# Expert 1's tokens in the later experts' order of d: quarter gathers and VectorE transposes for its second lot

## The chip, the cores and the metric

The kernel runs on one core of a Trainium2 chip. The metric is device time in microseconds (us), the median of several executions. One further execution was taken with the hardware profiler. Its trace is what "the profile" and "the trace" mean below, and its times count from the first instruction of the span.

Engines: TensorE (PE; its weight loads are PEld), VectorE (DVE), ScalarE (ACT), GpSimd (POOL) and SyncE (SP). SP issues the plain DMAs on a hardware queue. POOL issues the indirect DMAs (gathers and scatters by a list of indices) on a software queue.

## The reference

Two stages. Linear attention: for each of 8 batches and 8 heads, kv = kᵀv, out = q·kv, then a root-mean-square norm over the 64 channels of the head, times g_norm. The heads side by side are x, 8 x 576 tokens of 512 channels. Then a mixture of 8 experts in which each token goes to one expert:

```python
for b in range(B):
    prev_e = -1
    for s in range(S):
        fresh_e = int(np.argmax(logits[b, s]))
        if s == 0 or local_gate[b, s] < 0.5:
            e = fresh_e
        else:
            e = prev_e if prev_e >= 0 else fresh_e
        prev_e = e
        ...                      # p = softmax(logits[b, s])
        h = np.maximum(x[b, s] @ w1[e], 0.0)
        out[b, s] = p[e] * (h @ w2[e])
```

w1 is 8 x 512 x 1024 and w2 is 8 x 1024 x 512, all float32.

## The kernel before, in words

**Attention.** 16 steps of four batches' head pairs write unnormalised rows of x, with their norm factors and gates beside them, to a scratch tensor xs in DRAM: 4608 rows of 584 numbers, which are four pieces of 146, one for each pair of heads. The routing of each token is worked out beside it, and the tokens of each expert are listed (indices gidr for reading, sidr for writing).

**Experts.** The eight experts run one after another; "expert r" is the r-th in the order of work. Expert 0 has four blocks of 128 tokens, the last two each run by `block`. Experts 1 to 7 are sorted by their number of tokens on the chip, with fixed capacities WIDTHS (768, 704, 640, ...), so which weights expert r has is known only when `ranks` has run; SP then reads the numbers into registers (`read_ranks`, L1122) and issues the loads.

**Precision.** Each float32 product is three TensorE products: the operands are split into a high part (written by ScalarE) and a low part (by VectorE): high x high, high x low, low x high (`split_mm`, L961, L966, L967).

**Weights.** Each expert has four pieces of w1 and four of w2, of 512 KB. `wload` fetches a piece into one of four staging buffers `wst` (`wfetch`, L186 in the profile); `wsplit` has ScalarE write the high part (L233 for w1 with its scale g_norm, L230 for w2) and VectorE the low part (L234, L231), and then asks for the next load, which waits for a free staging buffer. The w1 pieces of expert 1 are called w_4 to w_7 in the profile.

**Tokens.** A block's 128 rows are gathered by POOL into a tile `xr` (six of them, XB, in turn), scaled by the norm factors (`scale`, L808), turned so that d lies on the partitions, and split into xh and xl. There are two ways to do this. A *whole* block is gathered by one DMA of whole rows (`gather`, L770), turned by four TensorE transposes into PSUM and split from there (`turn`, L820, L824, L825). The other way gathers a quarter of the row at a time (`gather4`, L780, four DMAs): quarter n of the partitions gets, in the u-th DMA, the u-th group of 32 tokens, piece by piece; VectorE then transposes 32 x 32 squares (`turn4`, L797) and the d index comes out in another order. The weights w1 must then lie in that order too (`quarters`), so their piece is read as four runs of 32 rows. Before the change, expert 1's blocks are whole and those of experts 2 to 7 are not.

**The order of work around the change.** Each of experts 1 to 7 has two lots of blocks, la and lb. Expert 1 has three blocks in each. For a lot, `first_wide` makes the first layer of all its blocks at once, in eight chunks of twelve products, with three PSUM buffers `ph`; ScalarE (L1031, hh) and VectorE (L1032, hl) take each chunk out. Then `second` makes the second layer block by block, ScalarE scales the result into one of two buffers `ot` (L996), and POOL scatters it to the output (L997). Lists of small jobs (`then`, `hooks`, `todo`) are written between the chunks: weight splits, scalings, turns of the next lot, and gathers of the lot after that, one per tick. For all engines but SP the program keeps the order in which it is written.

Expert 1's la is gathered, scaled and turned during `block` of expert 0's fourth block, and its w1 pieces are split there, at points given by its hooks. lb is gathered behind that, its blocks are scaled in the last three chunks of la's `first_wide`, and turned in la's second layer.

Of the kernel before, what the change touches and what calls it, by code (L numbers as in the profile page):

```python
# [11 lines left out]
I32 = mybir.dt.int32  # L12
# [10 lines left out]
def kernel(  # L23
# [12 lines left out]
    nc = tc.nc  # L36
    P = 128
# [69 lines left out]
    sidx = const.tile([P, KBM], I32, name="sidx")  # L107
    gidr = const.tile([P, NR * KBM], I32, name="gidr")

    gid4 = const.tile([P, NP, NR * KBM - KBM], I32, name="gid4")  # L110
    quart = const.tile([P, 2], F32, name="quart")
    own4 = const.tile([P, NP], F32, name="own4")
    nc.gpsimd.memset(own4, 0.0)
# [85 lines left out]

    def wload(e, i):  # L200
        t = wpools["w"].tile([P, 2 * DM], F32, name="wst", bufs=4)
        wfetch(t, by[e], i, e > 1)
        staged[e, i] = t

    by = {0: 0}
# [34 lines left out]
    def wsplit(e, i, two=False):  # L240
        t = staged.pop((e, i))

        if i < NW1:
            slot = (e * NW1 + i) % (2 * NW1)
            nm, pool = f"w1_{slot}", "s" if slot < NW1 else "b"
        else:
            slot = (e * NW2 + i - NW1) % (NW2 + 2)
            nm, pool = f"w2_{slot}", "scc"[slot] if slot < 3 else "d" if slot < NW2 else "b"
        hi, lo = (wtile(pool, nm + x) for x in "hl")
        low_ = split_w(hi, lo, t, i, e > 1)  # L250
        wt[e, i] = (hi, lo)

        def low(engine=nc.vector):
            low_(engine)
            if to_load:
                wload(*to_load.pop(0))

        if two:
            return low
        low()  # L260
# [388 lines left out]

    def by_quarter():  # L650

        n = NR * KBM - KBM
        pq4 = rbank[:, 128:128 + NP * n].rearrange("p (u n) -> p u n", n=n)
        for u in range(NP):
            nc.tensor.matmul(pq4[:, u], sel[0][:, u], trs[0][:, KBM:], start=True, stop=True)
        t = sm.tile([P, NP, n], F32, name="q4", tag="co")
        nc.vector.tensor_scalar(t, pq4, float(NP), quart[:, 1:2], op0=ALU.mult, op1=ALU.add)
        nc.vector.tensor_scalar(gid4, t, quart[:, 0:1], None, op0=ALU.max)
# [119 lines left out]
    def gather4(xr, c, u):  # L778

        i = nc.gpsimd.indirect_dma_start(  # L780
            out=xr[:, u * PW:(u + 1) * PW], out_offset=None,
            in_=xs.rearrange("t (q w) -> (t q) w", w=PW),
            in_offset=bass.IndirectOffsetOnAxis(ap=gid4[:, u, c - KBM:c - KBM + 1], axis=0),
            bounds_check=NT * NP - 1, oob_is_err=False)
        if behind:
            tc.add_manual_dep(i.ins, behind.pop().ins.name, mybir.DependencyInfo(
                mybir.DependencyClass.NoSync, mybir.DependencyReason.DATA))
# [3 lines left out]
    def pieces(xr, o=XO, n=P):  # L791
        return xr[:, 0:NP * PW].rearrange("p (a w) -> p a w", w=PW)[:, :, o:o + n]
# [22 lines left out]
    def turn(xr, xh, xl, t0, psum, tag="pt", pin=False, late=False):  # L815

        pt = psum.tile([P, ND, P], F32, name="pt", tag=tag)
        xv = pieces(xr)
        for d in range(ND):
            i = nc.tensor.transpose(pt[:, d], xv[:, d], ident)  # L820
            if late and not d:
# [463 lines left out]
    def remaining(some):  # L1285

        with tc.If(some > 0, preferred_fallthrough_block=True):  # L1287
            with ExitStack() as ov:
# [2 lines left out]
                tails(op, n0, KST)  # L1291
                others(op)

    class Block:


# [13 lines left out]
            return [lambda u=u: one(u) for u in range(NP)]  # L1310

        def scale(self):
            scale(self.xr)
            n = 1 if self.whole else NP
            t = xp.tile([P, NP, NR], F32, name="gs", bufs=2)[:, 0:n]
            nc.vector.tensor_mul(t, pieces(self.xr, XG, NR)[:, 0:n],
# [6 lines left out]

        def turn(self, xh, xl, t0):
            if self.whole:
                turn(self.xr, xh, xl, t0, ps_t)
            else:
                turn4(xp, self.xr, xh, xl, t0)

# [3 lines left out]
    def parts(r):  # L1333

        n = WIDTHS[r - 1]
        na = HM if n > 2 * HM - P else 2 * P
        bl = [Block(r, k, min(P, n - k * P), r == 1) for k in range(-(-n // P))]
        return bl[:na // P], bl[na // P:], na, n - na

    assert "F" in done  # L1340
# [26 lines left out]

    with tc.manual_schedule(engines=order):
        for bl in lb:
            bl.gather()  # L1370
        for r in range(1, E):
            la, lb, na, nb = lots[r]
            ma, mb_ = lots[r + 1][:2] if r + 1 < E else ([], [])
# [89 lines left out]
```

## Time and profile before

| | |
|---|---|
| median of three runs | 580.54 us (579.57 to 580.59) |
| the profiled execution | 575.91 us, of which the span is 574.1 us |
| busy share of the span | PE 94%, PEld 84%, DVE 53%, ACT 41%, POOL 40% |
| granted TensorE clock | 0.98 in the mean |
| DMA | 94.96 MB, 165 GB/s in the mean |
| instructions | 12792 |

A row of the timeline has its start and its duration in us, engine, line, operation, out<-in by the program's names, shapes, and in brackets how long the engine idled before it and what released it. A group's row has the count, and the least, median and greatest duration in ns. In a row of windows the busy times of PE, PEld, DVE, ACT and POOL follow the window's length, each with a count of instructions, and then come the granted TensorE clock, the share of the 16 DMA engines that was busy, and GB/s. A DMA queue's row has packets, MB, and its packets' time as a share of 16 engines. "issue" as a releaser means that the profile shows nothing that the engine waited for.

The attention part takes about the first 124 us, expert 0 the stretch to about 178 us, and experts 1 to 7 the rest.

### The profile page before, as it was taken

To read this page: it belongs to the slowest core of one execution; us is meant where nothing else is said; L and a number is where in the kernel's file an instruction comes from. 1 tells how busy PE (TensorE), PEld (TensorE's weight loads), DVE (VectorE), ACT (ScalarE), POOL (GpSimd) and SP (SyncE) were. 2 spreads that over 40 slices of the span, in tenths; PEclk is the share of its full clock that TensorE was granted. 3 is DMA by queue.
4 is the path that set the end of the run, shared out by engine and by line. 5 is a ranking of instruction groups with operands and counts; after the bars stand their busy time and mean duration, and the time that the engine had idled before them with its cause. 6 is when DMAs were issued, how large, how long until landed. Compare 5 with 4: busy or idle time off the path is not lost. (4 is left out here: it accounts for less than half of the span.)

```text
span 574.1 us, 12792 instructions
## 1 busy us (share of the span) xinstructions
PE 538.0 (94%) x5157; PEld 481.0 (84%) x5157; DVE 303.2 (53%) x627; ACT 237.6 (41%) x435; POOL 232.1 (40%) x303
## 2 busy tenths in 40 slices
PE   2977987789999999999999999999999999999996
PEld 2866876679878989898898898989798979999894
DVE  1126676699686525635463746374536545564510
ACT  1667766572254233332434343433433333435220
POOL 4224333161245527334353673447344634532001
PEclk9989889799999999999999999999999999999998
DMA  7999899980676354233343453336234533432000
GB/s 222 342 372 341 306 324 348 346 293 25 239 254 219 122 180 134 71 103 103 120 117 120 128 139 109 126 123 176 80 135 134 142 104 132 135 105 78 18 20 30
DMA packets 41379, 94.96 MB, mean 165 GB/s; under 512 B 7263, under 2 KB 7263, under 8 KB 41312
## 3 DMA queue, kind: packets, MB, share of 16 engines
q1 hardware_dynamic: 32032, 72.64, 37.1%
q0 software_dynamic: 7744, 21.41, 12.5%
q8 instruction: 42, 0.69, 0.5%
q10 hardware_dynamic: 1536, 0.02, 0.1%
q14 instruction: 25, 0.20, 0.1%
HBM read 73.85 MB, written 20.86 MB: 165 GB/s over the span
## 5 line engine op out<-in xcount | busy, mean ns | idle before, releaser
L780 POOL DMA_INDIRECT xr<-xs,gid x120 | 133.5, 1112 | 36.6 <-issue 33.2
L1032 DVE SCALAR_TENSOR_TENSOR hl<-ph,hh 128x384 fp32r<-128x384 f32 (+3 forms) x92 | 52.3, 569 | 113.6 <-ACT hh L1031 110.2
L997 POOL DMA_INDIRECT out_dram<-ot,sidr x34 | 33.8, 994 | 176.1 <-ACT ot L996 134.1
L1031 ACT ACTIVATE hh<-ph 128x384 fp32r<-128x384 f32 (+3 forms) x92 | 46.9, 510 | 121.7 <-PE ph L967 121.7
L996 ACT ACTIVATE ot<-py,pe 128x512 f32<-128x512 f32 (+1 forms) x37 | 25.4, 687 | 70.1 <-PE py L967 31.6
L495 POOL TENSOR_TENSOR sq<-raw 128x576 f32<-128x576 f32 x16 | 18.5, 1159 | 58.4 <-ACT raw L465 51.5
L375 PE MATMUL po<-vt,kt 64*64 64x64 f32 x1152 | 26.1, 243 | 15.7 <-DMA vt<-in_v_dram 11.5
L375 PEld LDWEIGHTS po<-vt,kt 64*64 64x64 f32 x1152 | 23.8, 156 | 14.3 <-issue 9.7
L500 DVE TENSOR_REDUCE ms<-sq 128x9 f32<-128x576 f32 x32 | 22.8, 747 | 21.5 <-POOL sq L495 19.5
L456 PEld LDWEIGHTS po<-kvb,qT 64*64 64x64 f32 x1024 | 22.2, 144 | 11.6 <-issue 9.3
L456 PE MATMUL po<-kvb,qT 64*64 64x73 f32 x1024 | 27.3, 242 | 4.7 <-issue 4.6
L462 ACT COPY raw<-po 128x876 f32<-128x876 f32 (+1 forms) x32 | 20.7, 651 | 15.3 <-PE po L456 15.1
L396 POOL COPY kvb<-kvp 64x128 f32<-64x128 f32 x64 | 20.5, 321 | 12.4 <-ACT kvp L379 10.0
L808 DVE TENSOR_TENSOR xr<-xr 128x512 f32<-128x512 f32 x37 | 25.4, 686 | 0.0
L801 ACT CAST yh<-xT 128x512 fp32r<-128x512 f32 x17 | 10.5, 620 | 29.5 <-DVE xT L797 29.4
L961 PE MATMUL py<-w_1h,hh 128*128 128x512 f32 (+1 forms) x56 | 22.2, 397 | 0.0
L435 PE MATMUL pq<-ident,qt 128*128 128x128 f32 x128 | 20.4, 307 | 1.8 <-issue 1.7
L966 PE MATMUL py<-w_0l,hh 128*128 128x512 f32 (+1 forms) x56 | 22.1, 395 | 0.0
L967 PE MATMUL py<-w_0h,hl 128*128 128x512 f32 (+1 forms) x56 | 22.0, 393 | 0.1
L961 PE MATMUL py<-w_0h,hh 128*128 128x512 f32 (+1 forms) x56 | 22.0, 393 | 0.0
L966 PE MATMUL py<-w_1l,hh 128*128 128x512 f32 (+1 forms) x56 | 21.9, 391 | 0.0
L967 PE MATMUL py<-w_1h,hl 128*128 128x512 f32 (+1 forms) x56 | 21.9, 391 | 0.0
(433 smaller groups left out, 1660.2 us busy)
## 6 DMA issues: line engine op xcount, KB each, us to landing
wst<-in_moe_w_dram SPq DMA_DIRECT2D x64, 512.0 KB, 3.7
xs<-raw SPq DMA_DIRECT2D x36, 292.0 KB, 4.4
kt<-in_k_dram SPq DMA_DIRECT2D x32, 288.0 KB, 4.6
vt<-in_v_dram SPq DMA_DIRECT2D x32, 288.0 KB, 4.9
qt<-in_q_dram SPq DMA_DIRECT2D x32, 288.0 KB, 5.5
xr<-xs,gid POOLq DMA_INDIRECT x120, 4.3
out_dram<-ot,sidr POOLq DMA_INDIRECT x36, 4.4
xr<-xs,gidr POOLq DMA_INDIRECT x6, 6.6
```

The costliest lines, as they stand in the source:

```text
L375: nc.tensor.matmul(pk[half(x ^ b), x, 0:D], ks[b][half(x), cd], vs[b][half(x), cd], start=(c == 0), stop=(c == C - 1))
L456: nc.tensor.matmul(po[half(b), r, o:o + HW], lhsT[half(r), half(x)], kvb[half(r), slot(x, b):slot(x, b) + HW], start=True, stop=True)
L500: nc.vector.tensor_reduce(mss[g][:, :, 2 * n + x], sqs.pop((s, x)), axis=AX.X, op=ALU.add)
L780: i = nc.gpsimd.indirect_dma_start(out=xr[:, u * PW:(u + 1) * PW], out_offset=None, in_=xs.rearrange("t (q w) -> (t q) w", w=PW), in_offse ...
L808: (engine or nc.vector).tensor_mul(xv, xv, r.unsqueeze(3).to_broadcast([P, NP, 2, D]))
L961: mm = nc.tensor.matmul(ps, ah, bh, start=(first and i == 0), stop=False)
L966: nc.tensor.matmul(ps, ah, bl, start=False, stop=False)
L967: nc.tensor.matmul(ps, al, bh, start=False, stop=(last and i == n - 1))
L996: nc.scalar.activation(ot[0:m], po[0:m], AF.Copy, scale=pe[0:m])
L997: return nc.gpsimd.indirect_dma_start(out=outf, out_offset=bass.IndirectOffsetOnAxis(ap=idx[0:m], axis=0), in_=ot[0:m], in_offset=None, bo ...
L1031: nc.scalar.activation(hh, ps, AF.Relu)
L1032: nc.vector.scalar_tensor_tensor(hl, ps[:, :, 0:nl], 0.0, hh[:, :, 0:nl].bitcast(F32), op0=ALU.max, op1=ALU.subtract)
```

## The change

Expert 1's first lot stays whole: gathered by whole rows and turned on TensorE. Its scaling now writes a second tile, with d put into the later experts' order on the way (`scale_turned`, two products of 256 elements for each block in place of one of 512). Its second lot is now gathered in quarters and turned on VectorE, as all later lots are. The w1 loads of expert 1 therefore come in four runs of 32 rows, and its split takes the scale vector in that order (gq for gcol). The table of quarter indices grows by the three blocks of lb (39 columns for 36).

```diff
-    gid4 = const.tile([P, NP, NR * KBM - KBM], I32, name="gid4")
+    gid4 = const.tile([P, NP, NR * KBM - HM // P], I32, name="gid4")
...
-        wfetch(t, by[e], i, e > 1)
+        wfetch(t, by[e], i, e > 0)
...
-        low_ = split_w(hi, lo, t, i, e > 1)
+        low_ = split_w(hi, lo, t, i, e > 0)
...
-        n = NR * KBM - KBM
+        n = NR * KBM - HM // P
...
-            nc.tensor.matmul(pq4[:, u], sel[0][:, u], trs[0][:, KBM:], start=True, stop=True)
+            nc.tensor.matmul(pq4[:, u], sel[0][:, u], trs[0][:, HM // P:], start=True, stop=True)
...
-            in_offset=bass.IndirectOffsetOnAxis(ap=gid4[:, u, c - KBM:c - KBM + 1], axis=0),
+            in_offset=bass.IndirectOffsetOnAxis(ap=gid4[:, u, c - HM // P:c - HM // P + 1], axis=0),
...
-        xv = pieces(xr)
+        xv = xr if len(xr.shape) == 3 else pieces(xr)
...
+    def scale_turned(xr):
+
+        t = xtile(xp, XB)
+        tv = t[:, 0:DM].rearrange("p (x y a i) -> p x a y i", x=2, a=NP, i=QD)
+        xv = pieces(xr).rearrange("p a (x y i) -> p x a y i", x=2, i=QD)
+        r = pieces(xr, XR, 2)
+        for x in range(2):
+            nc.vector.tensor_mul(tv[:, x], xv[:, x], r[:, :, x:x + 1].unsqueeze(3).to_broadcast(
+                [P, NP, DM // P // 2, QD]))
+        return t[:, 0:DM].rearrange("p (d k) -> p d k", k=P)
...
         def scale(self):
-            scale(self.xr)
+            if self.whole:
+                self.xs = scale_turned(self.xr)
+            else:
+                scale(self.xr)
...
-                turn(self.xr, xh, xl, t0, ps_t)
+                turn(self.xs, xh, xl, t0, ps_t)
...
-        bl = [Block(r, k, min(P, n - k * P), r == 1) for k in range(-(-n // P))]
+        bl = [Block(r, k, min(P, n - k * P),
+                    r == 1 and k < na // P) for k in range(-(-n // P))]
...
         for bl in lb:
-            bl.gather()
+            for what in bl.gathers():
+                what()
```

Three places show how instructions change or move. First SP, where expert 1's w1 loads are issued behind the reading of the ranks (wst is the staging buffer; the rows say the shape of the transfer, and the ISA rows between work out the address):

```order
 L1122 ISA x14
 L186 ISA
-L186 DMA wst<-in_moe_w_dram 128x1024
-L186 ISA
-L186 DMA wst<-in_moe_w_dram 128x1024
...
+L186 DMA wst<-in_moe_w_dram 128x1x1024
+L186 ISA
+L186 DMA wst<-in_moe_w_dram 128x1x1024
```

All four stand where they stood, in the same order, in the form that experts 2 to 7 have.

Second ScalarE, around expert 0's fourth block (h and hh are that block's hidden layer, w_4h to w_7h the high parts of expert 1's w1):

```order
-L233 ACTIVATE w_4h<-wst,gcol 128x1024
+L233 ACTIVATE w_4h<-wst,gq 128x1024
 L1075 ACTIVATE h<-ph 128x512
-L233 ACTIVATE w_5h<-wst,gcol 128x1024
+L233 ACTIVATE w_5h<-wst,gq 128x1024
 L1082 CAST hh<-pt 128x4x128
-L233 ACTIVATE w_6h<-wst,gcol 128x1024
+L233 ACTIVATE w_6h<-wst,gq 128x1024
 L1075 ACTIVATE h<-ph 128x512
-L233 ACTIVATE w_7h<-wst,gcol 128x1024
+L233 ACTIVATE w_7h<-wst,gq 128x1024
 L1082 CAST hh<-pt 128x4x128
```

Nothing moved; only the scale vector is another. The splits still alternate with the block's own steps.

Third POOL, from the gathers of expert 1 to its first output (gidr lists whole rows, gid quarters; sidx is the list of expert 0's fourth block, sidr that of the later experts):

```order
 L770 DMA xr_3040<-xs,gidx 128x584
 L997 DMA out_dram<-ot,si_2802 4608x512
-L770 DMA xr<-xs,gidr 128x584 x6
+L770 DMA xr<-xs,gidr 128x584 x3
 L997 DMA out_dram<-ot,sidx 4608x512
-L780 DMA xr<-xs,gid_88 128x146 x10
+L780 DMA xr<-xs,gid_88 128x146 x22
 L997 DMA out_dram<-ot,sidr 4608x512
 L780 DMA xr<-xs,gid_88 128x146 x2
```

The second lot's gathers, three before and twelve now, stood ahead of the fourth block's scatter and stand behind it.

## The prediction

> **What bounds the kernel now.** I read the page's busy shares first, then a window over the whole part with the experts, then TensorE's own idle rows. The page's first part; the window view over 178.4 to 568 us (columns: length, then busy time of PE, PEld, DVE, ACT, POOL, then clock, DMA share, GB/s); and TensorE's last wait of the timeline before that stretch:
>
> ```profile
> PE 538.0 (94%) x5157; PEld 481.0 (84%) x5157; DVE 303.2 (53%) x627; ACT 237.6 (41%) x435; POOL 232.1 (40%) x303
> ...
> 178.40:568.00 389.60, 389.60 (x2201) 352.08 (x2202) 194.76 (x350) 140.85 (x211) 169.17 (x156) 1.00 0.36 112
> ...
> 178.38 0.44 PE L966 MATMUL ph<-xl,w_4h 128*128 128x384 f32 x1 [0.29 <-DVE xl L825]
> ```
>
> From expert 1's first layer to the end TensorE is busy for 389.60 of 389.60 us at full clock. Whatever is taken off TensorE there is gained whole, and whatever makes it wait there is lost whole, since nothing later has room to give it back. The 0.29 us in the last row shows that expert 1's first layer starts as soon as its last block is turned. So its inputs, the turned blocks and the four first-layer weight pieces (w_4 to w_7), sit on the path already.
>
> ScalarE's timeline while the fourth block of expert 0 runs, where those pieces are split:
>
> ```profile
> 164.36 1.15 ACT L233 ACTIVATE w_4h<-wst,gcol 128x1024 fp32r<-128x1024 f32 x1 [0.20 <-issue]
> 166.16 0.60 ACT L1075 ACTIVATE h<-ph 128x512 f32<-128x512 f32 x1 [0.65 <-PE ph L967]
> 166.65 1.15 ACT L233 ACTIVATE w_5h<-wst,gcol 128x1024 fp32r<-128x1024 f32 x1
> 167.90 0.59 ACT L1082 CAST hh<-pt 128x512 fp32r<-128x512 f32 x1
> 168.38 1.15 ACT L233 ACTIVATE w_6h<-wst,gcol 128x1024 fp32r<-128x1024 f32 x1
> 169.44 0.58 ACT L1075 ACTIVATE h<-ph 128x512 f32<-128x512 f32 x1
> 169.91 1.15 ACT L233 ACTIVATE w_7h<-wst,gcol 128x1024 fp32r<-128x1024 f32 x1
> 171.45 0.59 ACT L1082 CAST hh<-pt 128x512 fp32r<-128x512 f32 x1 [0.39 <-PE pt L1080]
> ```
>
> The splits of w_4 to w_7 alternate with the fourth block's own steps (L1075, L1082), which TensorE waits for. A late piece therefore holds up not only the next expert but, through ScalarE's order, the block that runs now.
>
> **The loads.** SP's instructions in the changed kernel have expert 1's four first-layer loads in the form that experts 2 to 7 have already (128x1x1024 in place of 128x1024: four runs of 32 rows). The trace has both forms. SyncE's issues of expert 1 and of expert 2 (count; ns; first and last start), and the hardware queue (packets, MB, share of 16 engines) over 161.3 to 168.8, 185.6 to 209.2, 198.8 to 204.2 and 209.2 to 215.7 us:
>
> ```profile
> L186 SPq DMA_DIRECT2D wst<-in_moe_w_dram x4: 332/354/379, 160.3 to 162.0; - x4
> ...
> L186 SPq DMA_DIRECT2D wst<-in_moe_w_dram x4: 532/540/736, 183.4 to 189.7; - x4
> ...
> q1 hardware_dynamic: 576, 2.10, 73.7%
> ...
> q1 hardware_dynamic: 532, 2.07, 23.5%
> ...
> q1 hardware_dynamic: 132, 0.52, 24.3%
> ...
> q1 hardware_dynamic: 540, 1.08, 54.6%
> ```
>
> Expert 1's 2.1 MB pass in 7.5 us at 74% of the engines. Expert 2's, in quarters, need 23.6 us at 23.5%: with all four issued by 189.7, one 0.52 MB piece still takes 5.4 us alone at 24.3%, which is four engines of sixteen (0.25). So pieces in quarters run four wide and one behind the other. The second-layer pieces behind them (last row) are quick again. For experts 2 to 7 this is hidden, as the window above shows. For expert 1 it is not: the loads are issued at 160.3, when the ranks are known, and w_4h is wanted at 164.4.
>
> [...]
>
> From the first issue (183.4) to the end (209.2) are 25.8 us. The same from 160.3 puts the last piece at 186.1, and a quarter of the 23.6 us (5.9) between pieces puts the others near 168.4, 174.3 and 180.2. Bounds: four pieces alone, 4 x 5.4 = 21.6 after the same 2.2 us of start, give 184.1; expert 2's train had quarter gathers in its way, expert 1's will have three whole-row gathers, so up to 2.5 us (a tenth of the train) above 186.1, 188.6. I take 186.4 with the signal.
>
> Now ScalarE: w_4h at 168.7, L1075 behind it; w_5h at 174.6, the cast of hh behind it; w_6h at 180.5, the second L1075 at 181.7; w_7h at 186.4 instead of 169.91; the last cast of hh behind that. **Shift 16.5 us** (14.2 to 18.7). TensorE has nothing else: its order has the rest of this block, then expert 1. VectorE and TensorE at the end of that chain:
>
> ```profile
> 171.09 1.29 DVE L234 SCALAR_TENSOR_TENSOR w_7l<-wst,gcol,w_7h 128x1024 fp32r<-128x1024 f32 x1 [0.18 <-ACT w_7h L233]
> 172.29 0.68 DVE L1083 TENSOR_TENSOR hl<-pt,hh 128x512 fp32r<-128x512 f32 x1
> 172.90 0.68 DVE L808 TENSOR_TENSOR xr<-xr 128x512 f32<-128x512 f32 x1
> ...
> 173.10 0.44 PE L967 MATMUL py<-w_2h,hl 128*128 128x512 f32 x1
> ```
>
> w_7l follows w_7h, the block's hl follows w_7l, and the product at 173.10 is the first that needs it: it moves with w_7h by the whole 16.5. The four second-layer loads queue behind the train, but their splits follow the first layer of expert 1, some 6 us after that, and they move at twice the rate (last row of the queue), so I cost them at nothing; if they were 3 us late, ScalarE would lose that and TensorE with it.
>
> **TensorE's clock.** Before 186 TensorE sits idle from about 184.4 (the two transposed chunks and their products done) to 188, and for 3 to 5 us twice before. What a gap does, from the first part of this trace: the timeline's first matmul after a gap, and the windows behind two gaps of 1.72 us (clock is the third number from the end):
>
> ```profile
> 72.61 0.56 PE L456 MATMUL po<-kvb,qT 64*64 64x73 f32 x11 [1.72 <-issue]
> ...
> 55.70:62.50 6.80, 6.75 (x154) 6.42 (x155) 4.23 (x14) 4.32 (x10) 0.84 (x3) 0.50 0.88 304
> 72.70:76.10 3.40, 3.40 (x108) 3.27 (x107) 2.50 (x3) 2.20 (x3) 0.00 (x0) 0.50 0.84 277
> ```
>
> The clock was 0.50 for 3.4 or 6.8 us after it. Work of 5.3 us (173.10 to 178.38) then loses 1.7 to 3.4 us: **+2.5**, from 0 to 3.4. [...]
>
> **The turned blocks.** The first lot's scaling becomes two products of 256 elements with a new order. A 512-element one is 0.68 (row 172.90); one of 252 elements, also with a broadcast, is
>
> ```profile
> 142.68 0.41 DVE L556 TENSOR_TENSOR raw<-pe,se 128x252 f32<-128x252 f32 x1
> ```
>
> so two of them end 0.06 to 0.14 later per block, on the path: **+0.1**, and 0.4 if the new stride costs. The second lot loses three groups of four transposes on TensorE:
>
> ```profile
> 197.38 0.60 PE L820 MATMUL pt<-ident,xr 128*128 128x128 f32 x4
> 197.73 0.48 PE L961 MATMUL py<-w_5h,hh 128*128 128x512 f32 x1
> 198.04 0.39 PE L966 MATMUL py<-w_5l,hh 128*128 128x512 f32 x1
> ...
> 213.27 0.34 PE L961 MATMUL ph<-yh,w_4h 128*128 128x384 f32 x1
> ```
>
> From 197.38 to 198.04 are 0.66 us against 0.23 for the product alone: 0.43 each, **-1.3** for three. The three transposes on VectorE that replace them lie beside TensorE.
>
> **POOL.** Twelve quarter gathers replace three and stand behind the fourth block's output, 22 in a row ahead of expert 1's first output. The tiles they fill are the first lot's, read for the last time by its scaling, which precedes that output, so no wait comes from there. POOL's timeline, the gather's group (ns min/median/max), and that output's landing:
>
> ```profile
> 178.68 1.00 POOL L997 DMA_INDIRECT out_dram<-ot,sidx  x1 [4.13 <-ACT ot L996]
> 179.99 1.03 POOL L780 DMA_INDIRECT xr<-xs,gid  x1 [0.30 <-issue]
> ...
> 194.74 1.16 POOL L780 DMA_INDIRECT xr<-xs,gid  x1 [0.30 <-issue]
> 202.42 1.01 POOL L997 DMA_INDIRECT out_dram<-ot,sidr  x1 [6.53 <-ACT ot L996]
> ...
> L780 POOL DMA_INDIRECT xr<-xs,gid x120: 991/1000/1851, 180.0 to 507.9; - x120
> ...
> out_dram<-ot,sidr POOLq DMA_INDIRECT x1, 6.1
> ```
>
> In the clock of before: ten end at 195.9; twelve more at 1.30 (1.00 and 0.30 between) end at 211.5, with two or three slow ones at 213.5. The output goes then, not at 202.42, and lands 6.1 later, at 217.6 to 219.6. The buffer (two of them) is wanted by the third block's ot. ScalarE, with a case of such a wait, and VectorE:
>
> ```profile
> 213.52 0.69 ACT L996 ACTIVATE ot<-py,pe 128x512 f32<-128x512 f32 x1 [3.90 <-PE py L967]
> 215.56 0.49 ACT L1031 ACTIVATE hh<-ph 128x384 fp32r<-128x384 f32 x1 [1.35 <-PE ph L967]
> 217.63 0.49 ACT L1031 ACTIVATE hh<-ph 128x384 fp32r<-128x384 f32 x1 [1.59 <-PE ph L967]
> ...
> 310.45 0.58 ACT L1018 COPY ot<-py 64x512 f32<-64x512 f32 x1 [4.04 <-DMA out_dram<-ot,sidr]
> ...
> 216.08 0.56 DVE L1032 SCALAR_TENSOR_TENSOR hl<-ph,hh 128x384 fp32r<-128x384 f32 x1 [5.14 <-ACT hh L1031]
> ```
>
> Behind the late ot stands hh of the second lot's first layer. Three PSUM buffers let TensorE run three chunks of 2.07; it would want the fourth at 213.27 - 1.3 + 6.2 = 218.2 and gets it 0.69 + 0.49 + 0.56 after the landing, at 219.4 to 221.4, against 219.5 before. So the saved turns are eaten: net -0.1 to +1.9, **+1.0**; -1.3 if POOL is in time. The second lot's last gathers may also hold VectorE and the first ot by 1 to 2 us; that lies inside the same wait.
>
> **Sum** on the profiled execution (span 574.1, its time 575.9): 16.5 + 2.5 + 0.1 + 1.0 = 20.1, so 596.0. The median of the runs is 4.6 above it (580.5): **600.6 us**. Ends of the terms: 14.2 + 0 + 0 - 1.3 = 12.9 and 18.7 + 3.4 + 0.4 + 1.9 = 24.4, so 593.4 to 604.9.
>
> **Rivals.**
> Loads side by side: the four pieces on different engines, all landing about 168.7. For: nothing but that the queues look free at 161. Against: expert 2's, all issued by 189.7, still ran at 24%. ScalarE would then run w_4h to w_7h with the block's steps between, w_7h as late as w_4h (168.7 - 164.4 = 4.3); 4.3 + 1.1 = 5.4, no gap for the clock: 585.9.
> Loads hidden: the side of a gain. The place is w_7h; it decides when the train is over by 169.9, 9.6 us after its issue. Then -1.3 + 0.1 with POOL in time: 579.3; with POOL late, 0.1 + 1.0: 581.6, slower by the wait for ot alone. Against: 23.6 us in the only rows of that form.
> Worse: gathers slow each piece to 7.5 us, or the second-layer pieces come late too: 6 to 8 us more, 608.
>
> **How the numbers follow.** A measurement tells about 0.2% (1.2 us) from no change. Forecast 0.84; side by side 0.06; hidden 0.05 (a gain 0.03, nothing told 0.02); worse 0.05. Faster 0.03, same 0.02, slower 0.95. The range takes the ends of the terms and a little of the case with late second-layer pieces: 591 to 607.
>
> **What would show it.** Right: the hardware queue near 24% from 162 to about 186; w_7h near 186; idle TensorE in three pieces before it, half clock behind; no L820 in expert 1's second layer; 22 gathers ahead of an output, and a wait of the third ot for it. Wrong: w_7h before 175, or a queue share far above 25%.

## The result and the profile after

The changed kernel took 603.28 us (median of 4 runs, 600.25 to 604.37) against 580.06 (577.0 to 580.59, 4 runs) for the kernel before on the same chip: a ratio of 1.0403, 95% interval 1.0348 to 1.0459. That is 23.2 us slower, from 20 to 27 by the interval. The forecast was 600.6 in 591 to 607. Here and below a ratio leaves out executions more than 1.5% above the fastest of the same kernel, and a median does not. The profiled execution took 600.25, with a span of 598.4, against 575.91 and 574.1 before: 24.3 us more.

Of these 24.3 us, 4.4 lie ahead of everything that the change touches: expert 1's loads are issued at 164.71 instead of 160.31. The profiled execution of before was faster than all four of the runs above, and this part differs by some us from run to run (160.3 to 168.1 over all kernels below). So all that follows is counted from that issue. ScalarE's timeline of the changed kernel, the same stretch that the prediction shows of before:

```profile
174.04 1.15 ACT L233 ACTIVATE w_4h<-wst,gq 128x1024 fp32r<-128x1024 f32 x1 [5.46 <-DMA wst<-in_moe_w_dram]
175.09 0.58 ACT L1075 ACTIVATE h<-ph 128x512 f32<-128x512 f32 x1
182.90 1.15 ACT L233 ACTIVATE w_5h<-wst,gq 128x1024 fp32r<-128x1024 f32 x1 [7.23 <-DMA wst<-in_moe_w_dram]
183.96 0.57 ACT L1082 CAST hh<-pt 128x512 fp32r<-128x512 f32 x1
189.03 1.15 ACT L233 ACTIVATE w_6h<-wst,gq 128x1024 fp32r<-128x1024 f32 x1 [4.50 <-DMA wst<-in_moe_w_dram]
190.08 0.58 ACT L1075 ACTIVATE h<-ph 128x512 f32<-128x512 f32 x1
194.83 1.15 ACT L233 ACTIVATE w_7h<-wst,gq 128x1024 fp32r<-128x1024 f32 x1 [4.17 <-DMA wst<-in_moe_w_dram]
195.89 0.57 ACT L1082 CAST hh<-pt 128x512 fp32r<-128x512 f32 x1
```

None of the four splits waited for a transfer before; now each does, for 4.2 to 7.2 us, and directly behind each stands the step of the running block that TensorE needs. The last split starts 30.1 us after the first issue (194.83 - 164.71), where before it was 9.6 (169.91 - 160.31): 20.5 us. What TensorE waited for from 160 us on (the table of waits: total us, times, longest us), which was 0.8 us in all before:

```profile
PE py L961 <- ACT hh L1082: 8.5, 2, 6.3
PE pt L1080 <- ACT h L1075: 6.5, 2, 3.9
PE py L967 <- DVE hl L1083: 0.9, 2, 0.7
PE ph L961 <- DVE hl L1032: 0.9, 1, 0.9
```

The first three rows are the fourth block of expert 0, held up through ScalarE's order. The last is expert 1's second lot. The clock in this stretch, by windows (length, busy of PE, PEld, DVE, ACT, POOL, clock, DMA share, GB/s):

```profile
177.10:194.10 17.00, 7.84 (x19) 4.56 (x18) 3.17 (x3) 3.25 (x4) 0.00 (x0) 0.50 0.51 152
194.20:197.50 3.30, 0.85 (x3) 0.30 (x2) 1.49 (x2) 1.62 (x2) 0.00 (x0) 1.00 0.31 117
197.50:200.90 3.40, 2.95 (x10) 2.42 (x11) 2.85 (x11) 0.59 (x1) 0.00 (x0) 0.51 0.61 158
```

For most of it TensorE has half its clock, but there it waits for loads anyway; only the last window lies behind the last load. Where expert 1's first layer can go on with the last block's low part (below: "the first layer"; its very first product starts 0.7 us earlier), and TensorE's last product, after and before:

```profile
203.95 0.44 PE L966 MATMUL ph<-xl,w_4h 128*128 128x384 f32 x1 [0.28 <-DVE xl L825]
592.87 0.39 PE L967 MATMUL py<-w_1h,hl 128*128 128x512 f32 x1
```

```profile
568.43 0.39 PE L967 MATMUL py<-w_1h,hl 128*128 128x512 f32 x1
```

From the last split to the first layer are 9.12 us (8.47 before: +0.65), from there to the end of the last product 389.31 (390.44 before: -1.13). So counted from the issue: 20.5 + 0.65 - 1.13 = 20.0, and with the 4.4 ahead of it 24.4 of the 24.3 measured. The medians differ by 23.2, some 3 us more than these 20.0. The profiled execution was the fastest of the changed kernel's four, and the part ahead of the issue varies by more than 3 us, so it may hold the rest; no run shows that.

POOL, ScalarE and TensorE around expert 1's first output:

```profile
204.26 1.00 POOL L997 DMA_INDIRECT out_dram<-ot,sidx  x1 [30.44 <-ACT ot L996]
237.50 1.01 POOL L997 DMA_INDIRECT out_dram<-ot,sidr  x1 [0.30 <-issue]
...
242.76 0.69 ACT L996 ACTIVATE ot<-py,pe 128x512 f32<-128x512 f32 x1 [4.96 <-DMA out_dram<-ot,sidr]
...
244.47 0.44 PE L961 MATMUL ph<-yh,w_4h 128*128 128x384 f32 x1 [0.89 <-DVE hl L1032]
```

Between the first two rows POOL does 22 gathers (33.2 us), the output leaves at 237.50, the third ot waits 4.96 us for it to land, and TensorE stops once, for 0.89 us.

### The profile page after: what moved, and what is told of

It reads as the page before. It is cut to its first block, busy times and chain, and to the rows that moved or that the text cites. A ratio compares the mean times of both kernels' runs of the same rounds, so it can differ in the third digit from the quotient of the medians.

```text
span 598.4 us, 12799 instructions
## 1 busy us (share of the span) xinstructions
PE 543.0 (91%) x5145; PEld 482.7 (81%) x5145; DVE 306.8 (51%) x636; ACT 236.8 (40%) x435; POOL 243.8 (41%) x312
## 5 line engine op out<-in xcount | busy, mean ns | idle before, releaser
L780 POOL DMA_INDIRECT xr<-xs,gid x132 | 147.6, 1118 | 42.1 <-issue 39.7
L997 POOL DMA_INDIRECT out_dram<-ot,sidr x34 | 34.8, 1024 | 154.1 <-ACT ot L996 111.2
L375 PE MATMUL po<-vt,kt 64*64 64x64 f32 x1152 | 28.9, 249 | 17.3 <-DMA vt<-in_v_dram 12.6
L495 POOL TENSOR_TENSOR sq<-raw 128x576 f32<-128x576 f32 x16 | 19.7, 1231 | 60.3 <-ACT raw L465 56.8
L375 PEld LDWEIGHTS po<-vt,kt 64*64 64x64 f32 x1152 | 26.0, 162 | 18.0 <-issue 14.2
L456 PE MATMUL po<-kvb,qT 64*64 64x73 f32 x1024 | 28.7, 246 | 5.5 <-issue 5.4
L456 PEld LDWEIGHTS po<-kvb,qT 64*64 64x64 f32 x1024 | 23.6, 148 | 10.7 <-issue 6.1
L801 ACT CAST yh<-xT 128x512 fp32r<-128x512 f32 x20 | 12.4, 620 | 41.0 <-DVE xT L797 40.9
L808 DVE TENSOR_TENSOR xr<-xr 128x512 f32<-128x512 f32 x34 | 23.3, 686 | 7.3 <-DMA xr<-xs,gid 7.3
L396 POOL COPY kvb<-kvp 64x128 f32<-64x128 f32 x64 | 20.2, 316 | 15.3 <-ACT kvp L379 10.5
L797 DVE STREAM_TRANSPOSE xT<-xr 128x512 f32<-128x512 f32 x33 | 23.3, 706 | 0.5
```

Of the source, the lines that this page charges most:

```text
L375: nc.tensor.matmul(pk[half(x ^ b), x, 0:D], ks[b][half(x), cd], vs[b][half(x), cd], start=(c == 0), stop=(c == C - 1))
L456: nc.tensor.matmul(po[half(b), r, o:o + HW], lhsT[half(r), half(x)], kvb[half(r), slot(x, b):slot(x, b) + HW], start=True, stop=True)
L780: i = nc.gpsimd.indirect_dma_start(out=xr[:, u * PW:(u + 1) * PW], out_offset=None, in_=xs.rearrange("t (q w) -> (t q) w", w=PW), in_offse ...
L797: nc.vector.transpose(xT.rearrange("p j (u k) -> p u j k", k=QD), pieces(xr).rearrange("p u (j i) -> p u j i", i=QD))
L808: (engine or nc.vector).tensor_mul(xv, xv, r.unsqueeze(3).to_broadcast([P, NP, 2, D]))
L997: return nc.gpsimd.indirect_dma_start(out=outf, out_offset=bass.IndirectOffsetOnAxis(ap=idx[0:m], axis=0), in_=ot[0:m], in_offset=None, bo ...
```

## The experiments

Every run is compared with the kernel before on the same chip. The kernels ran on several chips, so beside the ratio the traces are compared by three stretches, whose ends are rows as shown above: from the first issue of expert 1's loads to the start of w_7h's split, from the issue to expert 1's first layer, and from there to the end of TensorE's last product. All in us, of one profiled execution each:

| kernel | issue | to w_7h | to the first layer | to the end |
|---|---|---|---|---|
| before | 160.31 | 9.60 | 18.07 | 390.44 |
| after | 164.71 | 30.12 | 39.24 | 389.31 |
| after, again | 167.82 | 30.66 | 39.41 | 389.16 |
| plain load | 166.82 | 9.58 | 17.78 | 388.92 |
| plain load, later gathers | 161.57 | 9.57 | 17.75 | 388.99 |
| quarter loads alone | 168.09 | 33.21 | 42.15 | 400.91 |
| gathers late | 163.85 | 27.18 | 41.06 | 399.89 |
| two runs a transfer | 164.97 | 50.18 | 59.66 | 398.09 |
| 32-row transfers | 164.82 | 15.23 | 24.37 | 398.89 |
| pairs of pieces | 163.41 | 15.28 | 23.41 | 389.11 |
| pairs, later gathers | 164.26 | 14.61 | 22.74 | 388.44 |
| pairs, other order | 161.30 | 14.55 | 22.68 | 388.42 |
| pairs, plain rows | 162.84 | 15.29 | 23.42 | 389.00 |
| halves, plain rows | 161.44 | 15.50 | 23.62 | 389.05 |

The theory was the prediction's: the loads in quarters run on four engines and set the end. The rivals were that the rest of the change costs as much, that the gathers or their order do, or that the form of the load is not what makes it slow.

**The load alone, and the change without it.** Two kernels split the change. The first is before with only the loads of expert 1 in quarters, the second is after with the plain loads. In both, expert 1's tokens meet its weight rows in another order than the reference's, with the same amount of work.

```diff
 # before, quarter loads alone
-        wfetch(t, by[e], i, e > 1)
+        wfetch(t, by[e], i, e > 0)
-        low_ = split_w(hi, lo, t, i, e > 1)
+        low_ = split_w(hi, lo, t, i, e > 0)
 # after, plain load: the same two lines the other way round
```

> The kernel before, with only expert 1's first-layer weights loaded as four runs of 32 rows, and their scale in that order; both lots stay whole and are turned on TensorE as before. Expert 1's tokens then meet weight rows in another order, so its outputs are not the reference's; the work is the same in kind and number. Theory: the load alone brings nearly all: 601 to 606 (the 23 us, plus 0.2 for what the rest of the change gave). The six whole-row gathers are all in the way of the train here, three of them more than in the changed kernel, so the train may be 2 to 4 us longer. Rival: 580 to 590.

> The changed kernel with expert 1's first-layer weights loaded and scaled as before (whole runs of 128 rows), all else as changed. The token rows of expert 1 then meet weight rows in another order, so its outputs are not the reference's; the work is the same in kind and number. What is left is the rest of the change alone. Theory (the load is the whole of the loss): w_7h as in before, and the rest by the changed kernel's trace: -1.3 for the transposes, +0.1 for the scaling, +0.9 for the wait for the third output's buffer: -0.3, so 0.997 to 1.002 of before. Rival (the first spread of the load stayed 11 us above before, of which w_7h explains 6; the rest of the change costs the other 5): 1.006 to 1.011.

The load alone: 1.0378 (1.0269 to 1.0488), from two of its four executions (604.05 and 611.46 us); the profiled one took 618.3, so only its load train is read from it below. The change without it: 579.43 us, 0.9976 (0.9941 to 1.0011). So the form of the four loads is the whole loss, and all the rest together lies between a gain of 0.6% and a loss of 0.1%. The waits of TensorE in the plain-load kernel, from 160 us on, and its last split:

```profile
PE ph L961 <- DVE hl L1032: 0.5, 1, 0.5
PE ph L966 <- DVE xl L825: 0.3, 1, 0.3
PE pt L820 <- issue: 0.3, 1, 0.3
```

```profile
176.40 1.15 ACT L233 ACTIVATE w_7h<-wst,gcol 128x1024 fp32r<-128x1024 f32 x1
```

The split waits for nothing, 9.58 us after the issue, as before. Only the short stop of the second lot is left. The changed kernel was run once more beside it:

> The changed kernel as it is, beside the two others on one chip. Theory: 1.035 to 1.046 of before as measured, so that the difference from the kernel with the plain load is the load's: 21 to 25 us. Rival (the load's share was 16 as forecast, and the rest of the change costs 5): a difference of 15 to 18 us.

It took 598.58 us, 1.0315 (1.0247 to 1.0383), which misses the expected interval from below by a little. Its trace has the same stretches as the first (30.7 and 39.4), so the load's loss is the same. The two profiled executions differ by 3.1 us (603.39 and 600.25), as do their first issues (167.82 and 164.71). Against the plain load it is 19.2 us slower by the medians, between what the theory (21 to 25) and the rival (15 to 18) expected; by the table it is 39.41 - 17.78 = 21.6 and 0.2 behind.

**Is it the width?** With two transfers of two runs of 32 rows for each piece, in place of one transfer of four runs, the same rows go by half as many engines, if the width goes by the runs.

```diff
+            if i < NW1 and quarters and type(quarters) is int and quarters == 1:
+                w = w1[e].rearrange("o (q j i) f -> j (o q) i f", j=NP, i=QD)
+                for n in range(2):
+                    fetch(t[n * 2 * QD:(n + 1) * 2 * QD], w[i, 2 * n:2 * n + 2])
```

> The changed kernel, with each of expert 1's first-layer pieces fetched by two transfers of two runs of 32 rows. If the number of engines follows the number of runs (two engines, the same two for all), one piece alone takes 10.8 us in place of 5.4, the train about 43 to 50 us, the queue's share is 12%, and the time 623 to 628. If what counts is the number of transfers or the length of one, or the engines differ from one transfer to the next, the train is as long as in the changed kernel or shorter: 590 to 604.

629.89 us in one execution, where before had a median of 584.9. ScalarE's splits:

```profile
183.16 1.15 ACT L237 ACTIVATE w_4h<-wst,gq 128x1024 fp32r<-128x1024 f32 x1 [14.34 <-DMA wst<-in_moe_w_dram]
193.15 1.15 ACT L237 ACTIVATE w_5h<-wst,gq 128x1024 fp32r<-128x1024 f32 x1 [8.36 <-DMA wst<-in_moe_w_dram]
204.26 1.15 ACT L237 ACTIVATE w_6h<-wst,gq 128x1024 fp32r<-128x1024 f32 x1 [9.49 <-DMA wst<-in_moe_w_dram]
215.15 1.15 ACT L237 ACTIVATE w_7h<-wst,gq 128x1024 fp32r<-128x1024 f32 x1 [9.26 <-DMA wst<-in_moe_w_dram]
```

The hardware queue over 185 to 193 us (packets, MB, share of 16 engines):

```profile
q1 hardware_dynamic: 104, 0.41, 12.7%
```

A piece every 10.0 to 11.1 us, against 5.4 for one alone on four engines, and 12.7% of sixteen engines, which is two of them (0.125). Four runs had 24.3% (expert 2's piece alone), so in these two forms the width is the number of runs. The two transfers of one piece do not run side by side either, or a piece would have taken half of that.

**Do the gathers slow the train?** The prediction's train had quarter gathers in its way, this one has the three whole-row gathers of the first lot. Here they are held back until w_7h is split (the helpers that keep the instructions at hand are left out):

```diff
...
-    for bl in la:
-        bl.gather()
+    def late_gathers():
+        wsplit(1, 3)
+        for bl in la:
+            bl.gather()
+            tc.add_manual_dep(bl.gins.ins, highs[-1].ins.name, mybir.DependencyInfo(
+                mybir.DependencyClass.Sync, mybir.DependencyReason.DATA))
...
-          {2: [split[0]], 4: [split[1]], 7: [split[2]], 8: [split[3]],
+          {2: [split[0]], 4: [split[1]], 7: [split[2]], 8: [late_gathers],
```

> The changed kernel, with the first lot's three whole-row gathers made to wait for the split of w_7h, so that none of them is in flight beside the train. In the changed kernel w_7h began 30.1 us after the first issue, where four pieces at 5.4 us and a start of 2.2 us make 24. Theory (the gathers' packets share the four engines and cost the train some 5 us): w_7h 24 to 25 us after the issue; the third gather then lands some 8 us behind w_7h, so the time moves by only -3 to +1: 600 to 604. Rival (the second-layer loads beside it, or the chip's memory, slow the train): w_7h stays 29 to 30 us after the issue, and the time rises by about 5.

611.8 us in one execution. The time says little, because the gathers are now late themselves, as VectorE's first scaling shows:

```profile
198.31 0.76 DVE L1303 TENSOR_TENSOR xr<-xr 128x256 f32<-128x256 f32 x2 [4.22 <-DMA xr<-xs,gidr]
```

The train answers the question: 27.2 us to w_7h with no whole-row gather beside it, 30.1 and 30.7 with three (after, twice), 33.2 with six (the quarter loads alone, whose second lot is gathered by whole rows too). So each such gather costs the train about 1.0 us (one trace each, but for the 30.1 and 30.7). The changed kernel's own queue agrees. Over 172.7 to 176.2 us, while the gathers' packets pass on POOL's queue, and over 180.7 to 184.7, behind them:

```profile
q1 hardware_dynamic: 43, 0.18, 15.9%
...
q1 hardware_dynamic: 97, 0.38, 25.6%
```

That is 51 GB/s for the train beside the gathers and 95 without. Neither side had the length right: the theory expected 24 to 25 us without gathers, the rival 29 to 30. But the rival named something that is there, the second-layer pieces. In this run SyncE issues the first two of them at 175.40 and 181.88, when a staging buffer comes free, and not behind the train, which lasts to 191. The queue over 179.8 to 181.8 and over 183.8 to 185.8 us:

```profile
q1 hardware_dynamic: 51, 0.21, 25.9%
...
q1 hardware_dynamic: 211, 0.47, 85.9%
```

The train has packets of 4 KB, the second-layer pieces have 2 KB (expert 2's before: 2.07 MB in 532 packets and 1.08 MB in 540). In the first window all the weights' packets are of 4 KB, in the second 33 of them. So the train lost about 0.7 us there (18 packets of 51 in 2 us), and as much beside the piece before: an estimate of 1.4 us for the two. Beside expert 2's train in the kernel before there was little of this, as its first such piece was issued at 207.4 and the train ended at 209.2. That is enough for the 1.0 by which 27.2 exceeds the 26 of expert 2's; no run holds these pieces back to prove it.

**A wider load with the same rows, in 16 transfers.** If the width goes by the slowest dimension, as 12.7% for two runs and 24.3% for four suggest, quarters of a piece (32 rows each) should go by more engines than four; that it would be all sixteen was the author's estimate (`quarters` carries the expert's number here and in the two-run kernel):

```diff
+            if i < NW1 and quarters and type(quarters) is int and quarters == 1:
+                w = w1[e].rearrange("o (q j i) f -> j q (o i) f", j=NP, i=QD)
+                for n in range(NP):
+                    fetch(t[n * QD:(n + 1) * QD], w[i, n])
```

> The changed kernel, with one thing else: each of expert 1's four first-layer weight pieces is fetched by four transfers of 32 rows in place of one transfer of four runs of 32 rows. Same rows, same places, same order. Theory (the form of the load is the cost: four engines of sixteen, one piece behind the other): the train of 2.1 MB is over about 8 to 10 us after its issue in place of 30, w_7h is split about 170 in the clock of before, and the time is that of before with the small terms: three groups of transposes less (-1.3), scaling in two halves (+0.1), the wait of TensorE for the third output's buffer that the changed kernel's trace shows (+0.9): 579 to 581, ratio to before 0.998 to 1.002. Rival (the twelve quarter gathers behind the fourth block's output, or the new scaling, carry a good part of the 23 us): 585 or more.

596.44 us, 1.0201 (1.0136 to 1.0266): half of the loss gone, but far from the 579 to 581 expected. Two things were wrong. The first is in the load:

```profile
169.95 1.15 ACT L237 ACTIVATE w_4h<-wst,gq 128x1024 fp32r<-128x1024 f32 x1 [1.27 <-DMA wst<-in_moe_w_dram]
...
180.05 1.15 ACT L237 ACTIVATE w_7h<-wst,gq 128x1024 fp32r<-128x1024 f32 x1 [2.29 <-DMA wst<-in_moe_w_dram]
```

15.2 us to w_7h instead of 9.6. SyncE's first eleven issues take 6.9 us (164.82 to 171.71), some 0.6 each; at that pace the sixteen take 10 of the 15.2 us, an estimate. The sixteen engines were little more than half busy, as the queue over 166.5 to 174.5 us shows:

```profile
q1 hardware_dynamic: 496, 1.35, 57.7%
```

The second lies behind the change, where TensorE stops, and the profile shows nothing that it waits for:

```profile
223.65 0.39 PE L970 MATMUL py<-w_1l,hh 128*128 128x512 f32 x1 [1.26 <-issue]
...
225.79 0.34 PE L965 MATMUL ph<-yh,w_4h 128*128 128x384 f32 x1 [1.02 <-issue]
```

From the first layer to the end this kernel took 398.9 us, against 388 to 390. But so did the three other kernels that ran on this chip (398.1, 399.9, 400.9), while all ten profiles on other chips have 388 to 390. One of the three, the quarter loads alone, has the code of before there, though its profile is of its slowest execution. So it looks like a matter of that chip and not of the edit, but it is not settled. The kernel before had a median of 584.9 there, 4 to 6 us above its medians elsewhere, but left no trace there, so the ratios of that chip may carry some of it.

**A wider load in 8 transfers.** With the four staging buffers in one tile, a transfer can take the same 32 rows of two pieces: 256 KB, half as many issues.

```diff
+        if not wsts:
+            wsts.append(wpools["w"].tile([P, 4, 2 * DM], F32, name="wst", bufs=1))
+        n = len(loads) % 4
...
+            w = w1[bass.ds(by[e], 1)].rearrange("o (q j i) f -> q (o i) j f", j=NP, i=QD)
+            for q_ in range(NP):
+                fetch(wsts[0][q_ * QD:(q_ + 1) * QD, n - 1:n + 1], w[q_, :, i - 1:i + 1])
```

> The changed kernel with the same rows in the same places, but expert 1's four first-layer pieces are brought by eight transfers of 256 KB, each with 32 partitions as its slowest dimension and two pieces in it (the four staging buffers are one tile for that). Theory (a transfer's width goes by its slowest dimension, and sixteen 128 KB transfers failed only by their number): the two pairs land some 6 and 8 us after the first issue, w_4h about 1.8 us later than in the kernel before, w_7h 1.3 to 1.5 us later; with the rest of the change worth -0.2% (the plain-load run) the ratio is 0.998 to 1.004. Rival (small transfers stay slow as they were in sixteen parts, 13 us for the four pieces): w_7h 4 to 6 us later, ratio 1.01 to 1.02.

582.91 us, 1.0050 (1.0015 to 1.0085): almost nine tenths of the loss are gone, but w_7h starts 15.3 us after the issue, not 11. That is the rival's pace for the load; the ratio lies between what the two sides expected. The issues are no longer the reason (eight within 4.0 us), and all sixteen engines are busy. The hardware queue (packets, MB, share of 16 engines) over 166 to 173 us of this kernel, and over 169 to 173 of the plain-load kernel:

```profile
q1 hardware_dynamic: 446, 1.48, 103.3%
```

```profile
q1 hardware_dynamic: 446, 1.63, 100.7%
```

Busy to the full in both, but 1.48 MB in 7 us are 211 GB/s and 1.63 MB in 4 us are 408. Sixteen engines writing 32 partitions, two pieces side by side, brought half (0.52) of what they brought when writing 128.

**Is it the partitions, or the rows?** Two kernels take the rows of the plain order, so again with expert 1's rows in another order than the reference's, through the same kind of transfers: eight onto 32 partitions, and four onto 64. Against the kernel of the pairs:

```diff
-            w = w1[bass.ds(by[e], 1)].rearrange("o (q j i) f -> q (o i) j f", j=NP, i=QD)
+            w = w1[bass.ds(by[e], 1)].rearrange("o (j q i) f -> q (o i) j f", j=NP, i=QD)
 # and for 64 partitions: i=2 * QD, and two transfers for a pair, each onto 2 * QD partitions
```

> The kernel of the pairs of pieces, with only the rows of HBM changed: the eight transfers still write 32 partitions and two pieces each, but they take the rows of the plain order, so expert 1's tokens meet its weight rows in another order than the reference's. In the run of the pairs a packet of 4 KB took 0.315 us, against 0.16 in the plain whole-piece loads, with all sixteen engines busy. Theory (the 32 partitions written at a time halve the pace): packets at 0.31 again, w_7h some 15 us after the first issue, time within 0.5% of the run of the pairs. Rival (the rows read set the pace): packets at 0.16, w_7h 9 to 11 us after the issue, 577 to 580 where the kernel before takes 580.

> The same plain rows in four transfers of 512 KB, each onto 64 neighbouring partitions and two pieces, so expert 1's tokens again meet its weight rows in another order than the reference's. If the pace goes with the number of partitions written at a time, 64 of them would bring most of it back: packets at 0.16 to 0.2, w_7h 10 to 12 us after the issue. [...]

One execution each: 582.54 and 581.1 us. The queue over 165 to 172 us of the first and 164.5 to 171.5 of the second:

```profile
q1 hardware_dynamic: 452, 1.47, 103.8%
```

```profile
q1 hardware_dynamic: 425, 1.55, 105.2%
```

210 and 221 GB/s (by these rows 0.32 and 0.31 us of an engine for each 4 KB, against 0.16 in the plain load), and w_7h after 15.3 and 15.5 us. The rows read didn't matter here (210 against 211), and 64 neighbouring partitions were hardly faster than 32. What no run excludes is that the two pieces side by side matter too: the one kernel with a single piece on 32 partitions, the sixteen transfers, was held by its issues.

**Can the order help?** Two kernels try what is left: fewer gathers ahead of expert 1's first output, with the plain load and with the pairs, and the pairs in an order that changes the half of the partitions at each transfer.

```diff
-            todo = [what for bl in ma for what in bl.gathers()]
+            todo = [lambda: None] * (NF if r == 1 else 0) + [what for bl in ma for what in bl.gathers()]
 # and, in the last one, also
-            for q_ in range(NP):
+            for q_ in (0, 2, 1, 3):
```

> As the kernel with the plain load, and the next expert's quarter gathers begin eight ticks later, so that 14 gathers and not 22 stand ahead of expert 1's first output on GpSimd. Outputs of expert 1 are not the reference's for the same reason. Theory: the first output goes some 10 us earlier, nothing waits for its buffer, and the time is 0.9 us below the kernel with the plain load, 0.995 to 1.000 of before. Rival (the gathers for the second lot, still twelve and behind the fourth block's output, hold VectorE and TensorE, not the output's buffer): no difference from the kernel with the plain load.

> The kernel of the pairs of pieces, with eight empty steps ahead of the quarter gathers, so that 14 and not 22 of them stand ahead of expert 1's first output. Theory (that order was worth about 0.2% with plain loads, 0.9957 against 0.9976, and the pairs cost about 1.5 us): 0.995 to 1.000 of the kernel before. Rival (the output's place is worth nothing once the loads come a little late): the same ratio as the run without the empty steps, 0.998 to 1.004; if the small transfers are slow, both 1.01 to 1.02.

> The kernel of the pairs with the empty steps, its transfers in another order: after the first quarter of partitions the third, then the second and the fourth, so that neighbouring transfers write different halves of the partitions. Theory (the engines go through one transfer after the other, so that two halves are hardly written together): packets stay near 0.3, and the ratio stays within 0.3% of that run's 1.0032. Rival (a transfer's end and the next one's start overlap by much): packets at 0.2 to 0.25, w_7h 2 to 4 us earlier, ratio 0.996 to 1.000.

Plain load, later gathers: 576.49 us, 0.9957 (0.9920 to 0.9994), against 0.9976 without the empty steps; the intervals overlap, so a gain over the plain load is not shown, and in the traces the stretch to the end is the same (388.99 and 388.92). The output left 45.4 us after the issue where it had left 51.2 after, 5.8 us earlier and not the expected 10, and it no longer stands behind gathers:

```profile
206.94 1.01 POOL L997 DMA_INDIRECT out_dram<-ot,sidr  x1 [5.21 <-ACT ot L996]
```

But one stop of 0.6 us is left, at a later place. With the pairs the stop went (388.44 against 389.11): 581.71 us, 1.0032 (0.9991 to 1.0072), against 1.0050: not the 0.995 to 1.000 expected, but what the rival said. By the traces the order is worth 0.7 us or less; the ratios, 0.2% apart in both cases, are within their intervals. The other order of transfers: 581.66 us, 1.0057 (1.0035 to 1.0079), w_7h after 14.55 us where 14.61 was; its queue over 163.5 to 170.5 us:

```profile
q1 hardware_dynamic: 494, 1.61, 103.6%
```

230 GB/s against 211: a little, as the theory said. How long neighbouring transfers overlap, no run shows. None of these kernels that computes the reference was faster than before.

## Why the prediction was right, and where its terms were not

The forecast was 600.6 and the time 603.28, slower as said, and for the reason given: the four loads in quarters are four engines wide (25.6% of sixteen, behind the gathers), and the change without them shows no loss (0.9976). The sum of 20.1 us met 20.0 in the trace, counted from the issue. That is partly luck, since three terms were off.

**The load train, +16.5 (14.2 to 18.7): 20.5.** The mechanism and the order were right: w_4h to w_7h late one after the other, each with a step of the block behind it. The step that was too small is the neighbours' price. "Up to 2.5 us (a tenth of the train)" for the gathers was kept as a bound, and only 0.3 of it taken; three whole-row gathers cost 2.9 to 3.5 us. And that the "four second-layer loads queue behind the train", at no cost, was wrong: the first three are issued at 176.53, 185.40 and 191.52, before w_7h's split, each when a staging buffer comes free. The train without gathers took 27.2 where 26.1 were forecast, and the pieces' estimate of 1.4 us covers that. A train measured with one kind of neighbour was carried to another kind without its price.

**TensorE's clock, +2.5, and the scaling, +0.1: together +0.65 and +0.3 in the two profiles of the change.** The half clock came as forecast (0.51 from 197.5 to 200.9), but it covered only 2.95 of the 6.0 us from the first product that needs the block's late hl to the first layer (197.95 to 203.95), and TensorE had room there. Before, the first and the third group of transposes (L820) start 0.58 and 0.61 us behind the product ahead of them, each as VectorE's scaling of its block ends; a group that waits for nothing starts 0.23 behind. Rows of before, then of after (rows between left out):

```profile
173.10 0.44 PE L967 MATMUL py<-w_2h,hl 128*128 128x512 f32 x1
173.68 0.62 PE L820 MATMUL pt<-ident,xr 128*128 128x128 f32 x4
...
175.74 0.40 PE L967 MATMUL py<-w_3h,hl 128*128 128x512 f32 x1
176.35 0.63 PE L820 MATMUL pt<-ident,xr 128*128 128x128 f32 x4 [0.22 <-issue]
```

```profile
201.72 0.39 PE L967 MATMUL py<-w_3h,hl 128*128 128x512 f32 x1
201.95 0.60 PE L820 MATMUL pt<-ident,xr 128*128 128x128 f32 x4
202.59 0.59 ACT L824 CAST xh<-pt 128x512 fp32r<-128x512 f32 x1 [0.55 <-PE pt L820]
203.21 0.69 DVE L825 TENSOR_TENSOR xl<-pt,xh 128x512 fp32r<-128x512 f32 x1 [0.44 <-ACT xh L824]
```

In after the scaling is done in time, the third group follows its product at once, xh waits for it and xl for xh: TensorE, late by the half clock, sets the pace. Half of 2.95 us is a loss of 1.5, an estimate, and the 0.7 us of room of before took part of it. From w_7h's split to the first layer are 8.47 us before, 8.20 in the plain load with no loss of clock, 9.12 and 8.75 in after. So the clock costs 0.6 to 0.9, not 2.5, and the scaling in halves nothing (-0.3 with its new order of steps). The working took the middle between one and two spells of half clock, where one came and only in part, and overlooked the room.

Which gap costs the clock the prediction took from the rows of before (gaps of 1.72 us, 0.50 behind them). The five kernels with pairs have one gap of over 1 us each in this stretch: after 2.77 us the clock stayed at full (1.00), after 2.95, 3.10, 3.28 and 3.63 it fell for about 3.4 us. In the first pairs kernel:

```profile
173.78 0.66 PE L1091 MATMUL pt<-ident,h 128*128 128x128 f32 x4 [3.28 <-ACT h L1086]
...
175.10:178.60 3.50, 3.50 (x10) 2.27 (x8) 1.85 (x3) 1.59 (x3) 0.00 (x0) 0.51 1.03 392
```

So here the clock fell after single gaps of 2.95 us and more, and not after one of 2.77; why it did after 1.72 in the first part was not tested. No run shows the lower end of this term, 0, at a gap as long as the 3.6 us forecast (3.63, in the halves, was followed by half clock): what the runs showed in its place is the 0.6 to 0.9 above. The price of a fall was small where TensorE had room.

**The turned blocks and POOL, +1.0 (-1.3 to +1.9): -1.1.** The order came as said: 22 gathers ahead of the output, the third ot waiting for its landing, hh behind it. The output left 33.2 us after the fourth block's, within the forecast's 32.8 to 34.8, and the third ot went on 5.3 later, not 6.1; TensorE stopped for 0.89 (0.6 in the second profile), not 1.2 to 3.2. And the three turns seem to have saved more than 1.3: without a stop, in two of the pairs kernels, the stretch is 388.4 against 390.4, 2.0. The value taken was at the wrong side of its range because each of its parts was taken from the slow side.

**The rivals.** "Loads side by side" and "loads hidden" fell with the train. "Worse" was half right in its cause (gathers slow the pieces, and the second-layer pieces do too) and wrong in its size (608).

**The experiments' misses.** That 32-row transfers would bring all back (579 to 581) left out the cost of issues, and that the pairs would (0.998 to 1.004) left out where the transfers write; both held to the width in engines alone.

## What to carry to other kernels

A transfer's shape set its speed twice here: by how many engines it was given, which followed the number of runs in its slowest dimension (12.7% of sixteen with two, 24.3% with four), and by how many partitions it wrote at once (211 GB/s onto 32, 408 onto 128); 128 partitions by sixteen engines was the only fast form of those tried. What ran beside the narrow transfers slowed them (51 GB/s beside the gathers, 95 behind them): find out what will be issued while they last. A layout that is free where loads are hidden can cost its whole length at the first place where a load is waited for (20.5 us here), so look at the wait of the first user before giving it an order that the later ones have. And before costing a stretch by an engine's busy time, see where the engine waits for another in it, since an engine that slows down can use up that room before it costs time: here the half clock cost 0.6 to 0.9 us where 2.95 us of it would alone be 1.5, an estimate.

## What the runs showed of the hardware that was not expected

Sixteen engines fully busy moved 210 to 221 GB/s onto 32 or 64 neighbouring partitions, 230 where the halves alternate, and 408 onto 128. A gather of 128 whole rows cost a four-engine train beside it about 1.0 us (27.2, 30.1 to 30.7 and 33.2 us with none, three and six). Four kernels on one chip took 398 to 401 us for the same work of experts 1 to 7 that took 388 to 390 on the others, with stops of TensorE, for some of which the profile shows no cause; that stays open.
